# Transposing attention weights with 128 instead of 120 weight columns, in a kernel whose work order is planned

## The chip, the core and the metric

The kernel runs on one core of a Trainium2 chip. A core has five engines with queues of their own: TensorE (PE in the profile, its weight loads are PEld), VectorE (DVE), ScalarE (ACT), GpSimd (POOL) and SyncE (SP, which here only issues transfers). The metric is the device time of one execution, in microseconds; lower is better.

## The reference

Two layers of each kind are interleaved on a sequence of 2048 tokens of width 512. The B layers are gated feed-forward layers of width 1792. The A layers are attention over segments of 32 tokens with 32 heads of 128, in which 8 memory tokens are carried from segment to segment:

```python
for s in range(n_seg):                                 # 64 segments, one after another
    xs = x[:, s * seg_len:(s + 1) * seg_len, :].copy()
    h = jnp.concatenate([mem, xs], axis=1)             # 8 + 32 = 40 tokens
    q, k, v = (einsum('btd,dhe->bhte', h, W) for W in (Wq, Wk, Wv))
    scores = jnp.einsum('bhqe,bhke->bhqk', q, k) * scale
    scores = jnp.where(mask[None, None], scores, -1000000000.0)
    p = _softmax(scores, axis=-1)
    o = jnp.einsum('bhqk,bhke->bhqe', p, v)
    o = jnp.einsum('bhte,hed->btd', o, Wo)
    mem = o[:, :M, :].copy()                           # memory for the next segment
    outs.append(o[:, M:, :])

x = x + A(layernorm(x));  x = x + B(layernorm(x))      # twice, with the same weights
```

(The lines are cut and joined; B is `(sigmoid(x w_gate) * (x w_up)) w_down`.) All data is bf16. The memory makes the segments of one A layer a sequence: segment s + 1 can't start before the output of segment s is there.

## The kernel before

**Steps.** The two A layers run interleaved. Step t treats segment t of the first A layer (job 0) and segment t - 6 of the second (job 1), so that there are 70 steps; steps 6 to 63 hold both jobs, the first six and the last six one alone. With both, 2 x 40 = 80 token columns are moved at once. After every fourth segment of a job, `ffn` treats the block of 128 tokens.

**Inside a step** (`emit_step`) the 32 heads come in six groups: four groups of six heads, one of six and one of two. A group of six of the first kind is two units of three heads; the fifth group is three units of two, the last one unit of two. For a group:

- Q and K are projected (L988), copied by ACT (L999, recorded at L1354) into `qku`, and multiplied to scores (L1023), keys of both jobs on 80 partitions.
- DVE adds the mask (L1037), takes the maximum (L1042), subtracts it (L1044); ACT takes the exponential (L1047); DVE sums (L1049), inverts (L1051) and multiplies (L1054) into `pb`, which is P: 80 rows, 40 columns a head.
- PE transposes P, one transpose a unit (`ptr`, L1067). The part of `pb` that is transposed is the stationary operand, so it is a weight load of 120 columns (three heads) or 80 (two heads); an identity of 80 columns is streamed past it.
- ACT or DVE spread the transposed rows into the block diagonal of `ptsb` (`spread`; L1346, L1348, L1354, L1356), the second and third head of a unit scaled by a column of `third`.
- PE multiplies `ptsb` by V (L1096) and the result by Wo into the bank WB (L1114), which all groups share.

**V.** The rows of V that don't depend on the memory are computed in blocks ahead of time (`v_pass` L778, `v_half` L815), copied into a staging tile and stored to DRAM (`scr`); each step loads the rows that it needs (L956, on SP) into `vsb`. The rest comes from `strips` (L902) by way of the staging tile `sst` (L968). At the start ("boot") the nine buffers of the feed-forward weights (`bootp`: wd, wg, wu) serve as staging tiles of 1024 columns, so that two pieces of 512 columns go into one tile (`k % 2`), with one store on SP or POOL (L793, recorded at L1350) behind the second.

**Order.** Everything is first recorded as a task: `pl.add(engine, cost, function, r=reads, w=writes, lat=...)`. `plan` runs a list scheduler over the 13,975 tasks: each has a cost in ns on its engine, `lat` is the time from its end (for a transfer, to its landing) until a user may go on, and at each moment an engine takes the ready task with the highest priority. The priorities are a list, `SEQUENCE`, packed in a string. The order that comes out is the order in which instructions are issued to each engine's queue; costs, latencies and planned times only shape that order. The waits in the program follow from which data the instructions touch. `warm` adds dummy matmuls where the plan has PE idle (L1340).

**Tiles.** `small` (61 fp32 columns) holds the layernorm sums, the softmax maxima and sums, `third` and other columns; `pb` (three buffers of 80 x 240) and `ptsb` (three of 128 x 680) are tiles of their own. `clear` sets `pb` and `ptsb` to zero once, on POOL.

Of the kernel before, what the change touches and what calls it, by code (L numbers as in the profile page):

```python
# [13 lines left out]
BF16 = mybir.dt.bfloat16  # L14
# [22 lines left out]
def mm_ns(n):  # L37
    return max(n / 2.4 + 2.5, 25.0)
# [23 lines left out]
;B75Pja>jU4U0pOM;*^MkbpH|%}4?Fg>}|j_Fe7An;0dBeihs~taRn~*1imyzs@MXBB0R9K{Dc(essuqm5vjVegY*#r;3xolo=*#1-?ZH8=!ZCdaFMf*a0}ivGjrbTwV#|upXo{Y+?axDr**4ycd`tV!a~o(^lb%  # L62
-d|rO0+fqgdAdzr&+KSQpq8AAQ0*bllqpd%tvRevJpxStQ^W4S_){6dW#yJY_W`r1E@FT2Uxe=|!7W;bJ)tl3672YV;FGR|DVkd^Z9mDZBU)|qz2vb)qec+qgR*uDfG(ABjQYg#!?>2ziThP3XJZ<7By}~T(MF*<
qmF#e8nAJ}ma5RRDM7n7!Nb*c#+B$l%NH_ohW(|Y6t=QIcKkF^gv<Ke0ElUlBE9Awhgg*r9z=q;UHs@XrLpn@^8STeZZpm4rYySV*A{`qe~i<=3=~}!a;!pmPIV4X0*myhJ8NM#8ZFT@lN3|sSL2RXU<MCM+=h3F
cUZtl1!cT4repZ2<a?7UOm;}eEcf1!9rU_qV9&joq!S>>G3~FaMh<O(&UUfQVJI;f>^4JS;D@BZ=ob$IV_U%(f}kMh?;ZR}K^`wxqux*PG;*O^h1ePrUE@nQ1@pKNjOnb@T<n5=h5Q7U)>ARO%)8N?R-z43f`hxu
+4<KMxhgcXLZh50zaR+``nWDvV-O3WIZ4Vj<BEn77tAgGG=~sz#LUy<|B#Lon1R^o_rI!MsvGkS_dZ78f4T}8IN#F-9wHSF%PIz7icWaJ4b@_n?S_W=>Fyp*`-u0QTY~^QPL=2~HW%F9o7rnLuhw{BDtJ}0wAvp*
>XmY-_MUDI?z*N!+72rFAXZww1+mn*!%y}5WMpwR?x4bSBcQK&1}P$VCH1FD^z*R7N_)S*T8UL7(59LW(nrkm+c3)tBWq(KN+pyFi}^NKK{Oc(695<~=YS=47k-}m!dOmUoc-~*P+Z(Y>tmXpp4aDvJ7r7p{1lSM
u9X|gIzGqGsuc|58KKIQH%j@r5l~dgqOrl|jnti3iaN8`w+vOj=t|+GmVm!O!ZRS?Gu%}Q*?|KbSryjiPzgVcoND-b??<=*mO{%qQ07lLnP}xvOB3Y{!~g4cdPK%7>L4i$Y9rV?tH%~;<YQ{`d#MMNH%)gPR&B$J
$Kx3;1Kalf&T2<)yrx~RW5hY=okh1t`vlxrVvm7*(t)*f-$TAkhr`S#w32=A#mr7Ibv|5zLDxLLRDU5561vE^wFhS`SYRnL#0jewffrZ2DBE1j^-aJG*6?H2hN_!{(Ya(cN+pX(4lOtXWOZ<KU%w4T+vAk+Q|CQr
+JBLZ@Wm?nY{e&+)JZS%pSix!b%<MckD^^LWV+rrcVgJ8Q-sqhLUDP)SDG&xeCUe%Ek_nkn$qR4%KI?Mhv9s2OAEmvMj$^-C`#gPbQCB7aZ%8(pvfa$lIZTnhji>N=Ve~^E}+mf#@;`5pK_R_ssCXTb72k6s!Qy2  # L70
Nl-HISA;yjHF-m>59MpPS`ebyqBOEi!Ep!qj@F3W5oWp5(6ZX2W73)u=ETUw$#LTVlLf<6eq2+Qy_sx*@txAt*NG(WJwNxh5P!7QZ6bNCaxLh@x&L6|Ad)L*Hh1yspW5K}ADaAn-2kQip}V9z1$;|e^_f_;d!7TQ
1%k?83~9`7E6Cm-Xr-(^DPf-`NN~2QW$OA%7a6z@+LtI)lwMqAl!t{ADJbWWFU<iWwp~cF`u)edOR%fWX_H>{O;(l`eGH3oa;~f(1nf0%0nu8BFCIdoIJ08c`}5%)^uV^DuFI(8$RYGbh0;Oo^394tSke1#G?bmu
kGfsucMtzFMi|ZuLu#Il4#rb*|J^r2YXt!mtOQW{MqE6cu1<LI;mw6g?O}g{lDqwgT+aa<GEfdx@xWPXYOIaMuK)I5oS4*~)XnW^Ke$*ys?)g;f8OyF{#6HCWyN)YduxAno>0aMm)lb7uZz#GEC+&lIY?76n#|L<
OA^MwN5<fyEuD4J3mv$dgbPa*N?*UwbVf_iq{zrI+&2J=GEIlma^Yfkb%cGcPCf<^(`85Iq=?w`??NAz#_l{>5xBr>!OVc)YBH`8>4Yd0d;{<pqm&=9DLbe0mz1Jyr^g)?_)s7j#W>-M9b?W60n-6cfWdAvGq*9Q
&Byd+WNK?rw+k@X#6qd?h{M;_aWm$*XQKfrX*eg?@~kI2&n3sYewY?T{J7(sA0E)TL?7wm);~OlR4ru7bF5g@1*yHpKKG_yB^}Z*ZH`*|0%H=2G)$Je6P8=zj}K$cDjNrBtIyjk=<&Z+b%M8M5H_@3mv`Y{gP4OR
4cgk}x2MybXqXI8T;wOVv1Hs>2dcRFe7<YS6H1^sMTYLrAL1|T&{PQ2u#T%->p&RQVaqpzMY{W3M7TZ0F<d0*d-rJTGYpAV9dKK!06|9hVvk_>Cz+%Or`;H6%?&+vXT36+a@PX0et1<EdwDr>Q|<OGRUZ-%hjEO}
k348PGh4Bv;N|)M=&8xnDp0=&@1#tSX_sF%ftuu^{mSsvt8dHG`nH2n90W>>+yHheyYv>3HONuWoPw8kQ@(vVmM+O#3#0#92G8s^>}(H$=f^uhUk^~=)zqJTmHw<|d<nld=($9vP~<$zkIr;(-dSI)isKvBw+ljE
?a*kR%(2jkH>AS4h}-*Sg_gCbZSof3D|Z696L#Q>Imqwe&G9_COS+DNZB0l%<@JyDGO(2n9@0W+;$8KNW{y{-r2k_|z4-^+HKJ8zo&3rHM<lJk;o@IvDp)ImjKu$izeCO$yW5DeRTvxU_jC5%%7R@}$+1*wMppQJ
U=;|4m@-@NYK=xqeE{58QTiDD%%W~wx1(RwuV5m&5|WeT5RCH<n*b#}!7e53%Lu{;VY}4e*(j{~dol)%DmpJZ8N6q2c*-j5v$smiOfbhQwxRG%D-CG5dlogMAoXm8$foMd`vL%<YafLq+;nd)l_y_qQwT#f<be}2
zh9_t_+Dc9wGv5|k>U+)*T%+zk`>YP!d(TBz7FV0e3earS;o28kDhG3luC&;i!cQ^*04vOS;kLcq?9a}rumn_uI6bWY}=MkLapbcf-z0_y0f40I>Kn0HH*aR{Fl~AVR3OO+ThgRV3L+3$4tPr)95L7TY7hAt0ebS  # L80
KGmY(!Jcq;A~dE+wRm1lKTqn2jb<&n-dV}dZ+`_;Jc}CQ<gn{cCW`Gq*E6UH$mFnRqt*7T#NbqTL3e}QD6-Oa0X%qw(_Y%aV$Lb<QRM__(w*3fPI&SO00BEv(c59EMNt+gaK4Zuf@ymO<-+##br*f+fH6-{dRBGY
9vKZ1&sa++b*<(=HJD9w<1lWjc2q>u{EI-k@WML0SbO2!;=TYsw`3+8xC~hG$WU`P&;*QSya^m&Ca|BQEmIYU++Crhl#+{j9q}$}i{WH0AGW=Fo2i%Y6Ew*4fPq4d%7i%tW6{H{Y3Wnq9Ol;IbUoUbwX4R4%bSsJ
&&gCiA()`I_M|Wx*}t|^Y<?)GV{M!j%#*{L5=~}SBA*^ge^h8DuP&c(ZR0ToFYP5;heN23-<56(4+|x{i($r&VIos5<JN5LmmET`ji0Z7PYNhY)My$?V@J15i%@eW<pJ+>qM_=T1h-w~&Q%HbC<F6{Tl^8Anp84u
7s;^7jAHamv&>I>*k<`gPKW+5+i1EMEl+pt6i*0`JM~fu8$oIaruqa9^Rg4a!O$*v{HIB;Bkyq79qz)^c+n8CvXEns6VE7EGf0{7%g;crn*d~S{n|0E3342om1T=7rFWc5Uawo7MwRZPy&i$hv|3dfH@w0;=f#F^
Z1tM;Uq$v9F|g08fm^yF6A}M`KL?YzqZ&N7D@Lc&_0A?v*S;?rj);Hp4yaArh8W4<I2oB#c~QkraeRi#I=ATf8~-U5lVKVo{3P_`H#xp=>;KbB>y)GV@A;%p_W!RMU+1Zp3R_e^eB<i1)x{D|hs}cw>E^%PtS^+3
2=+g+sowjML0P${9xg|CNN?kZVblt>M0(jn)$rYg<|YBK=o7Mz92~J`x`XV11L3FWsFL3Nu)k)vI_}N;szu!KN;CQ!i{D4!G2ZNL(>j-7nMG85h?l!bW2%D5l0?4GMBekT&_p9mG7n^iQbML~b7Daz?>CaVwURe*
l!B~;_{SE&z7shn<(Uz7F$fU0R@`bVqGQ&b+QU}70qYin9#f&?+PbR%&k&<{y&}~jdAGiee~dRVbYIY#n}Q&lX=m$05ah!)a(X*{EVR`&XJ>|Vz9ZoVcu-lZ1!l^nYh5OE^`X^L6`~jwZcTUCuM>&FaDr5(G)|%a
{pfOKR6Vhm!u>r6;^ZEB9)Ggz9-ku2u`j^IR#!>K3I9`*Ilz?+3NmSJ8C5zIxqRF*mvPTsU+wL2AGZxOKyw(}zx!Jjr}#D-l)gxA`wt2)tJv>RV}^X%7%zvCZSDiq?|0<2YSgL1z$Uu;M9@I`2$sxtO(aEW6IgOe
FUBMieS(?pPa!g`TN#==1r&TT>-fx&gCl?Xj8){T`x&yu`5us4XH3dY6%KIJK5$vS(rO~L<G?-ew|Vt?YB`3xZaz*RUONm$8&m`{Ks8;CfLbboJtYMr4rn}{I^stUcXyX~^e~z9l4SR%g&;>e>F(w~SeDg(aaQ2Z
&tD-Czi`2w<PI9*lEE!XVyv`;j#*(W<0(qftXYTpcLK46suXruoUI@$#{Qp9?omqCgCBjoFA#t+Lq&#8wXOtvDWJ38)|&~<Th_R}rn>h(({G<2uH|mHhP+QZ?@bG12C-;+29WEP)dCr<!jmF*d@ihJD>l3M%DD(Z  # L90
j+pZplYMEQK85F=Qd7Kx?EW?k62)~0L6MpRg>H2<@&rUT{%JBPfQ<g7;uul`l}X`MVkxeYN7McMYKD$0+2E8IqK5s6pCc7+CuOxpf|tkXtf)df6n!<^-G1Od%!hCaF#5H%p(6avkc|G~Bwf}arSSB7(hKsc<pulp
%_ZMqlc+l?ZNysSW-XO5a+HTDAaOuo$MOb1tc-^ky!_+NFn|VWwr;a{$e}9Pj(`_lhXUfW6P=zLtQWUX+zLOvaT88KEfQaY?Y|CFwL#3cunkY-Vteop$weuTdr01l8Q}IF^$9tZ-c?nmU#YM2g+3MXgwW#ynOAL0
m-9(pu0LF36=4$V)Xvxm4E48<Z7%+y8s~Oy7+BlYneIGy9l_Cj3|WF})i5qAtQ}@;(-aJ=O!%bQdu}w89-@6W9wG?GgtfO<2iLLV927-iSza1{BJwWok|+V%j8LfPAU-ci@6+G5W##{ds)Mmsa;p;5vRm!{c(kt_
!LEBmGgy#<uvgvRu$v1egBOO`lhZh)`Y^y=8?Z($VdV0U9)YMIz|66Q=$!SU+D+z}*EwH9lSAKT;w+(WyMWlV>I1MFFD-Z96gG$Lf1L*4pt-`XZcEo1e2;Mt(c$<I(6WD5ED}L5au!kM#21yBFU29PU-fU4@ey3G
&Lmeqv#lb^@Zo-VqurwOCu`(3q@G8Cu9=iO(fVRh-(+t&InT3Iowlxh+qF<5TR@yDyQ2eeC2JzC7DnCA@yG<uwXobge2yPgkoQYkx&V7CNd{#Txw)2kwM8`_81VG(2szd2gT#Vwub7-dD<%M2IAN5-QqpedJ>Mjy
a!x}}c)Nm|54q#BARV%X2a*L%0m*Fd(EPUXf91b-zLyOTp5-vth^6M2Et_{A*V|pEvJfx7R1X&M3mL0na&PF>BkUI}Mj)3#&I+$9H-D<S;XNnDx$$p%YGKHY9<ZkTF%1gt{c9`~jQ553WwJUP0ca}X8gg!Sc&<tc
TlD;(wxlQhW)>_8xJr=imo$q`Oxyg%oUKpATw79S`b&c*s9Q`8@pT%$EMtZbY|&B}COebJljqF&uUVW5jqZKZ3?#<iFF9L2oZKKDp_U96!4+NfOHe08^3LB`si{czzQU*IRCH8bAG`Bq0rT+=vbO!O|F>Q_euU>*
j%a|?kO7^s0~NOv+#S27_`A-+{Q6w#0Z=<B%Q@CdU<k`p`#*9!PY2p5kkO|l%x`SKXI~N~(Na)q_T0F23t+FTThf+4(n91#{AR`61#hDo<h0=aN}Ji_{yKb%fwrn49M@1{mV{n;t2O^q@CeS>Uwzr7)P9rMi&H;o
s~bdolUo?=aUpX?^S87FOj68T@c}Ru?HMraHa?+eR@WS&3)bOT|LNzR&u`wD!TCFYULJhzTP~RP|HQYEvt+t1;KP?eIuahlHr?xPf>#@B?*yj8NdX65F=#m^m@Z(I!unr;YwWP`rqpUlui`A37Bs#tE&%+Fp|>s|
D8XcEf|Hwg^(U7`-Z(KSsjXPX%A6hpZ+2>-htRfPzB&6+U3mrRBom^NBm;+6>zhA_2~71qP(LmnlXNW~t71T@MOyG)$4TViO~fxg4q)Nt9;E9JPMokhdzH|Y1Cp;FGCTc#%4?S~j%?lKP{@%Ky`7Ynd>cki!P%OO  # L100
2FF{spr}K29{qIn^~Ac*Y3pbraUP}zu)I<9)o1rl!~ncy(B}L7XCrv_84{n}SKBooG4s3d#gqIpGjb0?5xNBNI%XyZ#M_EvF}inxv*W?NSG66s-VWn0P0X<|Mp62mLFoN~Gr%IOiSNC>tJZ_)3Ku~$>mObw0MUnv
S;-B9Zrh7q#jzB~iVjW0ejWH_v7I{)?w+*3Rqg#+5y6HLS4t!_vDWUea^>lmqvLTgMAW)c@1)+x7#h%`?BbwiJ_N^DAWC4R-`411?e<0~9;)^?6hOsx5$+PRVm)&NYtnO<GR?z@g~s7h4p1R#f?at|6p%I{*+W{_
URx{&6s#4_h@RIy@2fU)rl3C5Ts~?LpQ~^&C7*h!Y(y~}$sSxQ;}HkK+VopD#EKUz)VM=r*n8ELu)DO*#yR>B(>K$LJlz6NLUY<R)TWCXK7xt?ymkH5G-*1(5%_(K$oL{4ZrDG918Eh?wS%_D@oR_C$p1M%@gnEZ
N~=6=Pim;h9#A)@I~r2*N1c*9q$0}1x<hL$F2-L-CAtVP$WMG0W}NBCAyhg0V6}1kJM1c8WPM~SOHorktqsd$Y*!oYOlux5Jpr?%`sP+>Ii@?a04RZ9u{237Gx@89qZ_1Iq66QjJU%GM{5~7#vK#wHB*9MkFx3HC
# [1315 lines left out]
```

## Time and profile before

| | |
|---|---|
| time, median of 3 runs | 1793.92 us (1793.05 to 1796.88) |
| the profiled execution | 1789.87 us, with a span of 1788.0 us from first to last instruction |
| PE, PEld busy | 1752.0 us, 1512.2 us |
| DVE, ACT, POOL busy | 1182.3 us, 1179.3 us, 578.6 us |
| granted TensorE clock, mean | 0.999 |
| transposes of P (L1067) | 840, of which 560 with 120 weight columns and 280 with 80 |

"Busy" is the time in which an engine had an instruction in work. Matmuls are pipelined, so that each one's duration (about 200 ns) is much longer than the distance to the next one's start; a matmul's cost in a dense stretch is that distance. A line of a group reads: line of the kernel, engine, operation, what it writes and reads, shape, count, then busy time in us and mean duration in ns, then the idle time of the engine ahead of it and what ended it.

### The profile page before, as it was taken

How to read it: one execution, taken by the hardware profiler on the slowest of the kernel's cores; microseconds unless marked ns; L12 is line 12 of the kernel's file. 1: busy time of each engine (PE TensorE's matmuls, PEld its weight loads, DVE VectorE, ACT ScalarE, POOL GpSimd, SP SyncE). 2: the span in 40 equal slices, each digit the busy share in tenths (PEclk: the TensorE clock that was granted, in tenths of full speed). 3: DMA queues.
4: the chain of work that ended last, by engine and by line, in shares of the span. 5: the costliest groups of instructions: out<-in, count | busy, mean ns of one | idle time of the engine just before them, and what ended most of it. 6: DMA issues, size and time to landing. Idle time of an engine off the chain costs nothing.

```text
span 1788.0 us, 91153 instructions
## 1 busy us (share of the span) xinstructions
PE 1752.0 (98%) x39103; PEld 1512.2 (85%) x39311; DVE 1182.3 (66%) x4076; ACT 1179.3 (66%) x3243; POOL 578.6 (32%) x837
## 2 busy tenths in 40 slices
PE   9999999999999999999999999999999999999998
PEld 4588788888888898989888898889888888889886
DVE  3367676776677667766776677667766765667675
ACT  4667777766666666666666666666666766666564
POOL 5412132422333242323324231333325231333432
PEclk9999999999999999999999999999999999999999
DMA  9735354634555463545546454556546454554543
GB/s 340 255 98 141 106 162 131 188 106 141 156 165 159 132 191 109 159 127 166 158 133 194 137 154 111 148 161 167 157 128 197 116 149 120 161 155 135 165 137 100
DMA packets 144752, 273.39 MB, mean 153 GB/s; under 512 B 34306, under 2 KB 82314, under 8 KB 144346
## 3 DMA queue, kind: packets, MB, share of 16 engines
q0 software_dynamic: 56720, 183.22, 35.1%
q1 hardware_dynamic: 87626, 84.31, 16.7%
q8 instruction: 308, 5.05, 1.2%
q14 instruction: 98, 0.80, 0.1%
HBM read 221.78 MB, written 27.07 MB: 139 GB/s over the span
## 4 chain that ended last, share of the span: by engine, by line
PE 89%; ACT 3%; DVE 2%; issue 1%; SPq 1%; DMA 1%; POOL 0%; DVEq 0%; ACTq 0%; POOLq 0%
PE bank L988 32%; PE bank L1114 17%; PE bank L1216 10%; PE bank L902 7%; PE bank L778 6%; PE bank L1023 4%; PE bank L1096 4%; PE bank L1239 4%; PE bank L1067 2%; PE bank L738 1%; DVE st L1037 1%; PE bank L1340 1%; SPq L968 1%; ACT ptsb L1346 1%; PE bank L1184 1%
## 5 line engine op out<-in xcount | busy, mean ns | idle before, releaser
L988 PE MATMUL bank<-hT,wq_sb 128*128 128x80 bf16 (+3 forms) x8960 | 615.5, 198 | 1.2
L988 PE MATMUL bank<-hT,wk_sb 128*128 128x80 bf16 (+3 forms) x8960 | 615.2, 198 | 0.8 <-issue 0.8
L1354 ACT CAST qku<-bank 128x480 bf16<-128x480 f32 (+3 forms) x770 | 380.7, 507 | 215.5 <-PE bank L988 185.1
L988 PEld LDWEIGHTS <-wq_sb 128*128 128x128 bf16 x8960 | 453.4, 99 | 23.3 <-issue 11.7
L988 PEld LDWEIGHTS <-wk_sb 128*128 128x128 bf16 x8960 | 447.0, 99 | 1.0 <-issue 1.0
L1037 DVE TENSOR_TENSOR st<-bank,cst 40x240 f32<-40x240 f32 (+3 forms) x768 | 278.9, 368 | 163.3 <-PE bank L1023 152.6
L1114 PE MATMUL bank<-otsb,wo_sb 128*128 128x80 bf16 (+1 forms) x8960 | 358.6, 198 | 1.6 <-ACT otsb L1354 0.2
L1114 PEld LDWEIGHTS <-wo_sb 128*128 128x128 bf16 x8960 | 336.5, 99 | 13.5 <-issue 0.9
L1209 POOL DMA_DIRECT2D wu<-in_B_w_up_dram x217 | 164.0, 756 | 273.6 <-PE bank L1216 126.5
L1208 POOL DMA_DIRECT2D wg<-in_B_w_gate_dram x217 | 163.9, 756 | 256.4 <-PE bank L1216 181.9
L1354 ACT CAST otsb<-bank 128x480 bf16<-128x480 f32 (+3 forms) x420 | 198.3, 483 | 52.3 <-PE bank L1096 35.4
L1233 POOL DMA_DIRECT2D wd<-in_B_w_down_dram x217 | 153.7, 709 | 207.4 <-PE bank L1023 71.8
L1346 ACT ACTIVATE ptsb<-bank,small 80x160 bf16<-80x160 bf16 (+5 forms) x477 | 169.5, 379 | 27.7 <-PE bank L1067 23.9
L1047 ACT ACTIVATE st<-st 80x240 f32<-80x240 f32 (+3 forms) x420 | 159.7, 383 | 29.0 <-DVE st L1044 25.6
L728 POOL TENSOR_TENSOR small<-small 128x1 f32<-128x1 f32 (+1 forms) x80 | 44.8, 563 | 402.1 <-DVE small L727 400.0
L1216 PE MATMUL bank<-xnT,wg 128*128 128x128 bf16 (+2 forms) x1784 | 172.0, 219 | 0.6
L1216 PE MATMUL bank<-xnT,wu 128*128 128x128 bf16 (+2 forms) x1784 | 171.0, 218 | 0.0
L1049 DVE TENSOR_REDUCE small<-st 80x6 f32<-80x240 f32 (+3 forms) x420 | 151.2, 362 | 24.5 <-ACT st L1047 22.8
L1023 PE MATMUL bank<-qku 128*128 128x80 bf16 (+1 forms) x2240 | 165.4, 198 | 0.7
L1044 DVE TENSOR_TENSOR st<-st,small 80x240 f32<-80x240 f32 (+3 forms) x420 | 154.4, 369 | 3.4
L1054 DVE TENSOR_TENSOR pb<-st,small 80x240 bf16<-80x240 f32 (+3 forms) x420 | 153.8, 369 | 4.2
L1042 DVE TENSOR_REDUCE small<-st 80x6 f32<-80x240 f32 (+3 forms) x420 | 151.8, 363 | 4.3
(104 smaller groups left out, 2405.3 us busy)
## 6 DMA issues: line engine op xcount, KB each, us to landing
wg<-in_B_w_gate_dram POOLq DMA_DIRECT2D x220, 256.0 KB, 4.4
wu<-in_B_w_up_dram POOLq DMA_DIRECT2D x220, 256.0 KB, 4.4
wd<-in_B_w_down_dram POOLq DMA_DIRECT2D x220, 256.0 KB, 4.3
vsb<-scr SPq DMA_DIRECT2D x345, 48.0 KB
vsb<-sst SPq DMA_DIRECT2D x372, 32.0 KB
scr<-vst SPq DMA_DIRECT2D x112, 96.0 KB
vsb<-scr SPq DMA_DIRECT2D x230, 24.0 KB
wv_sb<-in_A_Wv_dram SPq DMA_DIRECT2D x8, 512.0 KB
```

The costliest lines, as they stand in the source:

```text
L988: nc.tensor.matmul(o_ap, lhsT=W[:, c, h * P:(h + 1) * P], rhs=mv(c), start=(c == 0), stop=(c == DC - 1))
L1023: nc.tensor.matmul(s_all(SB)[:, w0 + i, :], lhsT=fview(qku[:, i, 0, 0:1], [(1, P)]), rhs=qku[:, i, 1, 0:ncol], start=True, stop=True)
L1037: pl.add("DVE", dve_ns(n, True), lambda gsz=gsz, hs=hs, st=st, SB=SB, pj_=pj_, npj_=npj_, mk=mk, idx=idx: nc.vector.tensor_tensor(out=st[p ...
L1044: pl.add("DVE", dve_ns(n), lambda gsz=gsz, hs=hs, st=st, mx=mx: nc.vector.tensor_tensor(out=st[pr, hs], in0=st[pr, hs], in1=mx[pr, hs].uns ...
L1047: pl.add("ACT", act_ns(n), lambda hs=hs, st=st: nc.scalar.activation(out=st[pr, hs], in_=st[pr, hs], func=ACTF.Exp, scale=self.scale), r=s ...
L1054: nc.vector.tensor_tensor(out=pb[pr, hs, 0:L], in0=st[pr, hs], in1=rs[pr, 0:gsz].unsqueeze(2).to_broadcast([npart, gsz, L]), op=ALU.mult)
L1114: nc.tensor.matmul(WB[:, c * ncol:(c + 1) * ncol], lhsT=self.wo[:, h, c * P:(c + 1) * P], rhs=otsb[:, hl, 0:ncol], start=(h == 0 and c == ...
L1208: pl.add("POOL", 760, lambda wg=wg, fs=fs: nc.gpsimd.dma_start(out=wg[:], in_=self.wgv[:, :, fs]), r=[("wo", self.H - 1)], w=[gk] + bt, la ...
L1209: pl.add("POOL", 760, lambda wu=wu, fs=fs: nc.gpsimd.dma_start(out=wu[:], in_=self.wuv[:, :, fs]), r=[("wo", self.H - 1)], w=[uk] + bt, la ...
L1216: nc.tensor.matmul(gu[:, 2 * i + k, 0:n], lhsT=W[:, c, i * P:(i + 1) * P], rhs=xnT[:, c, rw], start=(c == 0), stop=(c == DC - 1))
L1346: nc.scalar.activation(out=dst, in_=src, func=ACTF.Copy, scale=by)
L1354: nc.scalar.copy(out=dst, in_=src)
```

## The change

The tiles `small`, `pb` and `ptsb` become parts of one tile, `pbt`, of which each `pb` has 248 columns instead of 240. A transpose of three heads takes 128 columns of `pb` as its weights instead of 120: the eight further columns are the first of the next unit, or for the second unit the eight added ones, and the eight rows that come out more are not read. Transposes of two heads keep their 80 columns. In `v_pass` the first piece of a staging tile writes a key, and the second reads it, which puts the two in sequence in the plan. The stores of the boot are planned to land 6.0 us after their end instead of 5.0 us. The string `SEQUENCE` is replaced by another list of the same 13,975 tasks.

```diff
 SEQUENCE = r"""
-...
+...
 """
@@ setup_tiles
-        small = c.tile([P, 61], F32, name="small")
...
-        self.pb = [c.tile([LW, HG, L], BF16, name=f"pb{i}") for i in range(3)]
-        self.ptsb = [c.tile([P, 17 * L], BF16, name=f"ptsb{i}") for i in range(3)]
+        np_, nt_ = HG * L + P - 3 * L, 17 * L
+        pbt = c.tile([P, 3 * (np_ + nt_) + 2 * 61], BF16, name="pbt")
+        self.ptsb = [pbt[:, nt_ * i:nt_ * (i + 1)] for i in range(3)]
+        self.pb = [pbt[0:LW, 3 * nt_ + np_ * i:3 * nt_ + np_ * (i + 1)] for i in range(3)]
+        small = pbt[:, 3 * (np_ + nt_):3 * (np_ + nt_) + 2 * 61].bitcast(F32)
@@ v_pass
-            pl.add("PE", DC * mm_ns(512), vmm, r=keys + [("wv", h) for h in range(4 * k, 4 * k + 4)], w=[B], use=[vs])
+            own = ("own", len(pl.bufs)) if k % w == 0 else own
+            pl.add("PE", DC * mm_ns(512), vmm, r=keys + [("wv", h) for h in range(4 * k, 4 * k + 4)] + [own] * (k % w), w=[B] + [own] * (k % w == 0), use=[vs])
@@ v_pass and v_half, the stores
-                       ..., lat=3000.0 + 2000.0 * boot,
+                       ..., lat=3000.0 + 3000.0 * boot,
@@ emit_step, pmul
-                nc.vector.tensor_tensor(out=pb[pr, hs, 0:L], in0=st[pr, hs],
+                nc.vector.tensor_tensor(out=pb[pr, 0:gsz * L].rearrange("p (h k) -> p h k", k=L), in0=st[pr, hs],
@@ emit_step, ptr
-                pt = PB[0:w * L, 0:nu * LW // 2].bitcast(BF16)
+                m = P if w == 3 else w * L
+                pt = PB[0:m, 0:nu * LW // 2].bitcast(BF16)
                 for ul in range(nu):
-                    nc.tensor.transpose(out=pt[:, ul * LW:(ul + 1) * LW], in_=pb[full, w * ul:w * ul + w, :].rearrange("p i k -> p (i k)"),
+                    nc.tensor.transpose(out=pt[:, ul * LW:(ul + 1) * LW], in_=pb[full, w * L * ul:w * L * ul + m],
                                         identity=self.ident[full, full])
```

## The prediction

> **What bounds the kernel now.** I read the page first, then the stages, the groups by form, the timeline of one stretch, and the waits of the start. Page: span, busy time, and the shares of the chain that ended last.
>
> ```profile
> span 1788.0 us, 91153 instructions
> PE 1752.0 (98%) x39103; PEld 1512.2 (85%) x39311; DVE 1182.3 (66%) x4076; ACT 1179.3 (66%) x3243; POOL 578.6 (32%) x837
> ...
> PE 89%; ACT 3%; DVE 2%; issue 1%; SPq 1%; DMA 1%; POOL 0%; DVEq 0%; ACTq 0%; POOLq 0%
> ```
>
> PE is busy 98% and carries 89% of the chain. That alone doesn't say that a faster PE ends sooner, so I look at the stages (PE, PEld, DVE, ACT and POOL busy, granted clock, DMA share, GB/s):
>
> ```profile
> 0.00:100.00 100.00, 92.26 (x1082) 50.96 (x1094) 40.61 (x140) 54.87 (x138) 45.67 (x100) 0.98 0.85 283
> ...
> 300.00:1600.00 1300.00, 1284.88 (x28467) 1141.45 (x28631) 880.52 (x3010) 867.19 (x2260) 431.49 (x597) 1.00 0.53 151
> ```
>
> From 300 to 1600 us PE is busy 1284.9 of 1300 us at a clock of 1.00. As matmul durations overlap, I checked it by the distances from one matmul's start to the next's, over all records (distances that are a missing record of 216 ns left out). A 128x80 matmul with 128 columns of weights follows the last one after 35.8 ns, one of 128 columns after 56, one of 512 after 216. What exceeds these by over 40 ns is 16.8 us between 300 and 1600, 7.8 us in the first 100 us, 9.5 us from 100 to 300, and 8.0 us after 1600: 42 us in all. The long middle is a bare sum of PE's start distances; the two ends hold its waits.
>
> Next, weight loads by form (mean ns is the number ahead of the last bar):
>
> ```profile
> L1067 PEld LDWEIGHTS <-pb 80*120 80x120 bf16 x560 | 55.7, 134 | 9.6 <-DVE pb L1054 1.9 <-DVE st L1044 0.4
> L902 PEld LDWEIGHTS <-hT 128*32 128x32 bf16 x2272 | 54.1, 96 | 53.0 <-issue 1.7 <-DVE hT L1127 0.6 <-ACT oxT L1354 0.4
> L1096 PEld LDWEIGHTS <-vsb 80*128 80x128 bf16 x512 | 28.9, 98 | 5.5 <-issue 1.0 <-DMA vsb<-scr 0.2
> L1067 PEld LDWEIGHTS <-pb 80*80 80x80 bf16 x280 | 22.2, 118 | 4.2 <-DVE pb L1054 0.9
> L1239 PEld LDWEIGHTS <-hff 128*96 128x96 bf16 x14 | 1.4, 122 | 1.7 <-DVE hff L1222 1.1
> ```
>
> 32, 80, 96 and 120 columns take 96, 118, 122 and 134 ns: (134 - 96) / 88 = 0.43 ns a column. 128 columns lie off that line, at 98 ns on the same 80 rows. The reader is to see that the 560 loads of P (four groups of heads, two transposes each, 70 steps) are the slowest form of the table, by 36 ns. Whether that reaches the end shows in the timeline of PE (start, duration):
>
> ```profile
> 804.84 0.27 PE L1023 MATMUL bank<-qku 128*128 128x80 bf16 x3
> 804.94 0.28 PE L1067 MATMUL bank<-cst,pb 80*120 80x80 bf16 x2
> 805.05 0.32 PE L988 MATMUL bank<-hT,wq_sb 128*128 128x80 bf16 x4
> 805.20 0.31 PE L988 MATMUL bank<-hT,wk_sb 128*128 128x80 bf16 x4
> ```
>
> Three score matmuls take 0.10 us to the next start, the two transposes 0.11 us, although all stream 80 columns.
>
> Last, the waits between 36 and 58 us (us in total, times, longest), and the landing of the start's V stores:
>
> ```profile
> ACT wg L1354 <- DMA scr<-wg: 5.5, 1, 5.5
> ACT wd L1354 <- DMA scr<-wd: 4.7, 1, 4.7
> PE bank L778 <- ACT xvf L1354: 3.5, 1, 3.5
> PE bank L778 <- ACT wg L1354: 1.0, 1, 1.0
> ```
>
> ```profile
> DMA to landing us min/median/max: 2.0/5.3/7.2
> ```
>
> Twice ACT stands before a copy into a staging tile whose old store hasn't landed. V banks then stay full, and PE stops: start distances exceed theirs by 1.19 us at 40.7 and 3.62 us at 53.7, half of what the first 100 us lose. The plan reckons with 5.0 us to landing; half of the stores need more than 5.3.
>
> **The change, part by part.** The sum is made on the profiled execution (1789.87 us for a span of 1788.0). The median of the runs shown is 1793.92, 4.05 us above; I carry the difference to the median.
>
> **Transposes of threes.** Nothing is added: 560 loads of 120 columns become loads of 128, the matmul still streams 80 columns. Bound above by the slope of the slow rows: 8 x 0.43 = 3.4 ns, x 560 = 1.9 us slower if 128 columns stay slow. Below, by the row of 80 rows x 128 columns (L1096): its 80-column matmuls follow each other after 36.2 ns in mean. The 548 transposes that have a next record within 60 ns of theirs lose 7.55 us against 35.8 ns, 13.8 ns each: the second of a pair starts 50 ns after the first (median), the next instruction 55 ns after the second. Against 36.2 ns it is 7.3 us, for 560 some 7.5 us. Here two sections of "TensorE: Matmul & The Clock Gate" in the Trainium skill differ. "LDWEIGHTS" gives a time in proportion to the columns alone, P / 1.2 ns, which speaks against the change: an estimate of 6.7 ns for 8 columns, 3.7 us over 560, slower. "Weight-path perf modes" says that a fast load is taken when there are exactly 128 weights and the type isn't FP32, which gives the 7.5 us faster. The rows decide for the second (98 ns on the same 80 rows against 134). What no row shows is a 128-column load from an odd place: the new pb buffers begin every 496 bytes, the second transpose 240 bytes on; the 128-column loads shown start at multiples of 64 bytes in their tiles. [...]I keep the near row.
>
> How much reaches the end: 5.1 us of it lies between 300 and 1600, where PE waits 16.8 us in 1300; I count 0.9, as a step's hand-over (the transposes of L1184 wait on ACT for the last oxT) doesn't shorten with PE. The other 2.4 us lie where a step alone waits for its own chain: three quarters. 4.7 + 1.8 = **6.5 us**.
>
> The eight new output rows are read by nobody (L1346 to L1356 still take 120). POOL clears 248 columns a buffer instead of 240, beside the first weight loads: nothing.
>
> **One tile for pb, ptsb and small.** Same instructions and bytes. The risk is a wait between parts that don't overlap. The nearest case is small itself: POOL writes one part of it (L728), DVE others 420 times each (L1042, L1049, L1051), and line 1042 shows no idle time ahead of it at all. cst is shared likewise. So nothing; if regions were not told apart, DVE's P would wait for the transposes of another group, 420 times at a fraction of a us, over 100 us. I leave that out of the range.
>
> **Pieces in sequence, stores later.** The "own" key adds no instruction and no wait, only an order in the plan: nothing by itself. The longer landing (6.0 us, above the median of 5.3, below the longest of 7.2) makes the plan pick another staging tile or do other PE work first. At best both stops go, 4.8 us. But the DMA engines are busy 0.85 in that stretch, and a tile used later pushes a V piece, its ACT copy and its SP or POOL store back. If no PE work is ready in its place, nothing is won, and one more wait like that of 1.19 us, or two, may come: +2. Between -4.8 and +2 I take **-3 us**, near the end that the trace names. Next late after this would be V rows from DRAM (297.5 us: 1.7 us of PE).
>
> **Another order.** Every priority is rewritten. Decoded and set against the order that the plan of before gives, PE's tasks between 200 and 1600 us move by one place in the median (nine of ten by up to 6), those of the first 100 us by 26, of the second by 9, after 1700 by 5. ACT and POOL look alike, DVE moves by 5 to 10 places throughout; SP's loads and stores move by 1 to 3 places in the median, nine of ten by under 20. So the middle stays, and start and end are laid anew. It can win a part of the 9.5 + 8.0 us that PE waits there, and lose as much; nothing in the trace of before shows which: **0**, +-4.
>
> Sum: 6.5 + 3 = 9.5 us; 1793.92 - 9.5 = 1784.4, told as **1784**.
>
> **The rivals.** Where PE waits anyway, a faster PE only waits more. *Hidden:* if the steps of the middle were bound by the chain through DVE and ACT, the transposes would give a third, 2.5 us, and the start 3: 1788.4. For it: L1184 waits of 0.5 us at block ends. Against: 98.8% busy there, DVE and ACT 68 and 67%. *Slow load:* odd addresses or 80 rows deny the fast load: 1.9 us lost, 3 won, 1792.8. For it: no such address in the trace. Against: 98 ns on 80 rows. *Order wins:* a laid-anew start and end give back 8 of their 17.5 us beyond the stop at 53.7: 1776.
>
> *Slower:* SP's queue is in order, and carries V's stores (L1350) as well as the loads of V rows that the P times V matmuls (L1096) await (L956, L968). If the new order puts loads behind stores that wait for their copy, these rows come late. The chain shows what one costs: "DMA vsb<-sst" at 295.85 us, of which PE lost 1.71. Such stops must use up the 6.5 us first (the start then wins nothing), and 3.6 more; from six new ones on it is slower by over 0.2%, at seven 1793.9 - 6.5 + 12 = 1799.4. Against it: SP's order moves by 1 to 3 places in the median, and only three such waits stand among the longest pieces of the chain.
>
> **How the numbers follow.** 0.2%, 3.6 us, is about what a measurement of this kernel can tell from no change. The forecast 0.62 (0.02 of it within 0.2%), order wins 0.12, hidden 0.12 (0.02 within), slow load 0.06 (all within), slower 0.08. Faster 0.60 + 0.12 + 0.10 = 0.82, same 0.10, slower 0.08. The range takes full gain and order (7.5 + 4.8 + 4 = 16.3, a little more for order wins: 1775) and the slow load's 1792.8, so 1775 to 1793; outside lie the slower case and the tail of order wins.
>
> **What would show it.** Right: P's loads of threes at 98 ns instead of 134, the transposes' distances near 36 ns, PE busy between 300 and 1600 as high as now with that stretch's work done some 5 us sooner; ACT's waits on scr<-wd and scr<-wg gone before 60 us. Wrong: loads at 137 ns; the same 98 ns but PE's waits grown by 5 us; new waits on vsb<-scr or vsb<-sst; waits between DVE pb and ACT ptsb that share no data.

## The result, and the profile after

| | before | after |
|---|---|---|
| time, median | 1793.07 us (1784.54 to 1797.11, 20 runs) | 1788.57 us (1786.39 to 1793.41, 20 runs) |
| the profiled execution | 1789.87 us | 1789.13 us |
| PE's weight loads of three heads, mean of one | 134 ns | 99 ns |
| ACT busy | 1179.3 us | 1201.9 us |

The ratio is 0.998, interval 0.9971 to 0.999: the changed kernel is faster by 0.2%, some 3.6 us of 1793 (the medians lie 4.5 apart). The forecast was 9.5 us. The time lies in the range, the direction is right, and more than half of the gain is missing. The two profiled executions differ by 0.7 us only, because the one of before was 3 us quicker than its median; they serve to see where time goes, the ratio to say how much.

The page of the changed kernel, its span, busy times and the shares of the chain that ended last:

```profile
span 1787.1 us, 91201 instructions
...
PE 1765.1 (99%) x39305; PEld 1505.1 (84%) x39305; DVE 1184.6 (66%) x4075; ACT 1201.9 (67%) x3244; POOL 579.0 (32%) x837
...
PE 90%; ACT 4%; DVE 3%; DMA 1%; issue 1%; SPq 1%; DVEq 0%; POOL 0%; ACTq 0%; POOLq 0%
```

PE still sets the time. (That it is busier by 13 us says little: the trace of before holds 39,311 weight loads but 39,103 matmuls, so some 200 matmul records are missing there; here both are 39,305.) The number to stop at is ACT's. Its work is nearly the same copies and spreads (3244 instructions against 3243), and it is busy 23 us longer.

The stages (PE, PEld, DVE, ACT and POOL busy, granted clock, DMA share, GB/s):

```profile
0.00:100.00 100.00, 96.90 (x1266) 55.49 (x1267) 47.39 (x165) 63.15 (x169) 46.54 (x101) 1.00 0.87 289
...
300.00:1600.00 1300.00, 1291.98 (x28499) 1131.30 (x28495) 880.56 (x2994) 879.47 (x2242) 426.82 (x591) 1.00 0.53 150
```

In the first 100 us PE is busy 96.9 us instead of 92.3 and passes 1267 weight loads instead of 1094: the start is denser. The granted clock of these 100 us is 1.00, where before had 0.98; the experiments come back to that. In the middle there is 12 us more of ACT, and 136 weight loads *fewer* in the same 1300 us. So the start gains, and the middle gives back.

The weight loads of P by form, and the start's waits of ACT for staging tiles (us in total, times, longest):

```profile
L1033 PEld LDWEIGHTS <-pbt 80*128 80x128 bf16 x560 | 40.8, 99 | 12.8 <-DVE pbt L1019 4.0 <-DVE st L1009 0.4
L1033 PEld LDWEIGHTS <-pbt 80*80 80x80 bf16 x280 | 22.0, 118 | 4.9 <-DVE pbt L1019 2.2
```

```profile
ACT wg L1320 <- PE bank L742: 2.0, 6, 0.4
ACT wd L1320 <- PE bank L742: 1.8, 5, 0.5
ACT wu L1320 <- PE bank L742: 0.9, 3, 0.5
ACT wg L1320 <- PE bank L780: 0.7, 1, 0.7
ACT wu L1320 <- DMA scr<-wg: 0.3, 1, 0.3
```

The loads of 128 columns take 99 ns instead of 134, although they begin at odd places. The two waits of 5.5 and 4.7 us for V's stores are down to one of 0.3 us. Both things that the prediction reckoned on have happened. Something else costs time, and it shows in ACT's timeline. Two spreads of three heads, one right behind the other, are one entry "x2"; start and length of the pair stand in front. First a pair of before on ACT and one on DVE, then after:

```profile
703.18 0.67 ACT L1346 ACTIVATE ptsb<-bank,small 120x160 bf16<-120x160 bf16 x2
...
747.43 0.50 DVE L1348 TENSOR_SCALAR ptsb<-bank,small 120x160 bf16<-120x160 bf16 x2
```

```profile
699.82 0.81 ACT L1312 ACTIVATE pbt<-bank,pbt 120x160 bf16<-120x160 bf16 x2
...
744.15 0.63 DVE L1314 TENSOR_SCALAR pbt<-bank,pbt 120x160 bf16<-120x160 bf16 x2
```

A pair takes 0.14 us longer on ACT and 0.13 us on DVE. The groups hide it, because an instruction's own duration has not changed (line, engine, operation, shape, count | busy, mean ns | idle before, releaser), before and after:

```profile
L1346 ACT ACTIVATE ptsb<-bank,small 120x160 bf16<-120x160 bf16 x172 | 66.8, 392 | 7.5 <-PE bank L1067 6.1 <-DVE ptsb L1356 0.5
```

```profile
L1312 ACT ACTIVATE pbt<-bank,pbt 120x160 bf16<-120x160 bf16 x176 | 68.9, 395 | 7.6 <-PE bank L1033 3.8 <-DVE pbt L1016 0.3 <-DVE pbt L1322 0.2
```

392 and 395 ns. In before, two durations of 392 fit in 0.67 us, so they overlap by some 0.11; in after two of 395 take 0.81, with no overlap left. I therefore measured, over all spreads that directly follow a spread on their engine, the distance from the end of the one to the end of the next (medians in ns; 160 columns are a spread for both jobs):

| | before | after | e3_pack_only | e5_ptsb_apart |
|---|---|---|---|---|
| ACT, 120x160 | 290 | 426 | 427 | 291 |
| ACT, 80x160 | 280 | 422 | 423 | 290 |
| ACT, 40x160 | 172 | 317 | 318 | 173 |
| DVE, 120x160 | 208 | 337 | 336 | 208 |
| DVE, 40x160 | 143 | 267 | 267 | 142 |

(The last two columns belong to the experiments.) The cause stands in the program. Among the instructions that spread, ACT has 325 of 752 that wait for an earlier instruction of *ACT itself*, where before had 26 of 737; on DVE it is 96, where before had none. In before two spreads write two tiles, or parts of one tile that the program tells apart. In after all three `ptsb`, all three `pb` and `small` are parts of one tile, and the spreads get waits on each other.

The trace of after separates the two kinds within this one tile, when an engine's instructions are set beside the program's in order. Of the 98 spreads of 120x160 on ACT that follow a spread, the 89 with a wait on ACT end 426 ns after it (median), the 9 without such a wait 284 ns. On DVE all 59 of 160 columns have the wait; the spreads of 40x80, of which none has it, stay at 102 ns as in before.

### The profile page after: what moved, and what is told of

Read it like the earlier page. It is cut to its first block, busy times and chain, and to the rows that moved or that the text cites. A ratio compares the mean times of both kernels' runs of the same rounds, so it can differ in the third digit from the quotient of the medians.

```text
span 1787.1 us, 91201 instructions
## 1 busy us (share of the span) xinstructions
PE 1765.1 (99%) x39305; PEld 1505.1 (84%) x39305; DVE 1184.6 (66%) x4075; ACT 1201.9 (67%) x3244; POOL 579.0 (32%) x837
## 3 DMA queue, kind: packets, MB, share of 16 engines
q1 hardware_dynamic: 87658, 84.38, 16.8%
## 4 chain that ended last, share of the span: by engine, by line
PE 90%; ACT 4%; DVE 3%; DMA 1%; issue 1%; SPq 1%; DVEq 0%; POOL 0%; ACTq 0%; POOLq 0%
PE bank L953 31%; PE bank L1080 16%; PE bank L1182 10%; PE bank L742 7%; PE bank L867 7%; PE bank L1205 5%; PE bank L988 4%; PE bank L1062 4%; PE bank L1033 2%; ACT pbt L1312 1%; PE bank L1306 1%; DVE st L1002 1%; PE bank L702 1%; ACT qku L1320 1%; PE bank L1150 1%
## 5 line engine op out<-in xcount | busy, mean ns | idle before, releaser
L1320 ACT CAST qku<-bank 128x480 bf16<-128x480 f32 (+4 forms) x770 | 379.7, 507 | 211.4 <-PE bank L953 173.4
L1312 ACT ACTIVATE pbt<-bank,pbt 80x160 bf16<-80x160 bf16 (+4 forms) x488 | 181.6, 381 | 27.5 <-PE bank L1033 18.0
L692 POOL TENSOR_TENSOR pbt<-pbt 128x1 f32<-128x1 f32 (+1 forms) x80 | 45.3, 568 | 391.3 <-DVE pbt L691 390.7
L1014 DVE TENSOR_REDUCE pbt<-st 80x6 f32<-80x240 f32 (+3 forms) x420 | 151.4, 363 | 29.9 <-ACT st L1012 27.3
L1009 DVE TENSOR_TENSOR st<-st,pbt 80x240 f32<-80x240 f32 (+3 forms) x420 | 154.5, 369 | 3.3
L1019 DVE TENSOR_TENSOR pbt<-st,pbt 80x240 bf16<-80x240 f32 (+3 forms) x420 | 153.8, 369 | 4.3
L1007 DVE TENSOR_REDUCE pbt<-st 80x6 f32<-80x240 f32 (+3 forms) x420 | 151.9, 363 | 4.2
```

What stands on the lines that cost most here:

```text
L1009: pl.add("DVE", dve_ns(n), lambda gsz=gsz, hs=hs, st=st, mx=mx: nc.vector.tensor_tensor(out=st[pr, hs], in0=st[pr, hs], in1=mx[pr, hs].uns ...
L1019: nc.vector.tensor_tensor(out=pb[pr, 0:gsz * L].rearrange("p (h k) -> p h k", k=L), in0=st[pr, hs], in1=rs[pr, 0:gsz].unsqueeze(2).to_broa ...
L1312: nc.scalar.activation(out=dst, in_=src, func=ACTF.Copy, scale=by)
L1320: nc.scalar.copy(out=dst, in_=src)
```

## The experiments

Theory W: the one tile adds waits of ACT and DVE on their own earlier work, and these eat the gain. Rivals: O, the other order loses in the middle what it wins at the start; H, a transpose that is done sooner shortens nothing there. The four kernels ran on one chip beside before, whose median on it was 1797.0 us (1791.53 to 1803.86, 17 runs). Percentages are ratios to before, and us are per cents of 1797.

### e3_pack_only: before, with the one tile and nothing else

The order, the landing time and the transposes are those of before; `pb` has its 248 columns, of which a transpose takes 120. As an edit of the changed kernel (cut):

```diff
-                m = P if w == 3 else w * L
+                m = w * L
 SEQUENCE, lat and keys: as before
```

> The kernel before with pb, ptsb and small as parts of one tile, and nothing else: 120 weight columns, old order, old landing. In the program 302 spreads on ACT and 100 on DVE then wait for an earlier instruction of their own engine. Theory W (these waits eat the gain; after, one ACT spread ends 420 ns behind another in place of 285): slower than before by 3 to 7 us, 1796 to 1800. Theory O (the new order in the middle eats it) and theory H (the middle is bound by the softmax chain anyway, so a faster PE only waits more): no change, 1793 +-1.5.

Measured: 1809.87 us (1805.23 to 1814.17, 6 runs), ratio 1.0063 (1.0038 to 1.0088): **slower by 0.6%, some 11 us**. PE, SP and POOL get the same instructions in the same order with the same waits as in before; only the waits of ACT on ACT and of DVE on DVE differ. O and H have nothing to say to such a loss. W has the right sign and too small a size. The pair of spreads, and then the stage of the middle:

```profile
710.79 0.81 ACT L1349 ACTIVATE pbt<-bank,pbt 120x160 bf16<-120x160 bf16 x2
...
757.02 0.63 DVE L1351 TENSOR_SCALAR pbt<-bank,pbt 120x160 bf16<-120x160 bf16 x2
```

```profile
300.00:1600.00 1300.00, 1275.45 (x28056) 1128.04 (x28218) 877.73 (x2982) 874.65 (x2229) 424.34 (x588) 1.00 0.53 149
```

The same 0.81 and 0.63 us, and PE gets through 28,218 weight loads in the 1300 us instead of 28,631. What PE waits for fits spreads that end later. First before, then e3_pack_only (us in total, times, longest):

```profile
PEld L1096 <- issue: 5.6, 10, 1.7
...
PEld L1067 <- DVE pb L1054: 2.8, 9, 0.5
...
PE bank L1096 <- DMA vsb<-sst: 1.8, 2, 1.5
```

```profile
PEld L1099 <- issue: 11.3, 32, 1.7
...
PE bank L1099 <- DMA vsb<-sst: 7.4, 5, 2.6
...
PEld L1070 <- DVE pbt L1056: 4.7, 17, 0.5
```

Transposes wait more often for DVE's P, and P times V (L1099), the user of the spread rows, twice as long. ("issue" names no releaser, so that it is the spread which holds P times V is argued, not shown.) The rows of V by way of `sst` come late too; I take it that the step's timing has shifted against its loads.

### e1_t128_old_order: the one tile and the wide transposes, in the old order

As an edit of the changed kernel (cut):

```diff
 SEQUENCE: as before
-                       ..., lat=3000.0 + 3000.0 * boot,
+                       ..., lat=3000.0 + 2000.0 * boot,
-            own = ...; r=... + [own] * (k % w), w=[B] + [own] * (k % w == 0)
+            r=..., w=[B]
```

> The change without its plan: 128 weight columns and the one tile, with the old order, no sequence key and the old landing. W: the transposes' 6.8 us less what the one tile costs, 1790 to 1794. O: 1786.5, the full gain of the transposes, as the old order fits. H: 1790 to 1792, a third of it.

Measured: 1801.82 us (1797.83 to 1808.47, 12 runs), ratio 1.003 (1.0014 to 1.0045): slower than before by 0.3%, with the fast weight loads in it. Against e3_pack_only it is 0.33% faster, 6 us by the ratios and 8 by the medians: the wider transposes pay even here, which speaks against H, and less than the tile costs.

### e5_ptsb_apart: the changed kernel, with the spreads' targets as tiles of their own

Everything of the change stays, the order too; only the three `ptsb` leave the shared tile. (To make room, `small` is cut to 54 columns: the layernorm's reciprocal is written over sums that are no longer needed, and three constants lie in spare columns of the third `pb`. So `pb` and `small` still share a tile.)

```diff
-        pbt = c.tile([P, 3 * (np_ + nt_) + 2 * 61], BF16, name="pbt")
-        self.ptsb = [pbt[:, nt_ * i:nt_ * (i + 1)] for i in range(3)]
+        self.ptsb = [c.tile([P, 17 * L], BF16, name=f"ptsb{i}") for i in range(3)]
+        pbt = c.tile([P, 3 * np_ - 8 + 2 * 54], BF16, name="pbt")
```

> The changed kernel with ptsb as three tiles of its own (pb and small share one, two columns of the layernorm sums are reused in place): no spread waits for its own engine, PE's and SP's programs are the same as after's. W: faster than after by 3 to 7 us, 1782 to 1785.5. O and H: like after, 1788.5 +-1.5.

Measured: 1780.98 us (1778.67 to 1783.44, 6 runs), ratio 0.9906 (0.9886 to 0.9926): **0.9% faster than before**, and the fastest kernel here. PE, SP and POOL have the programs of the changed kernel down to the waits, and the spreads' waits on their own engine are back at before's 26 on ACT and none on DVE. So O falls: the same order that had won 0.2% wins 0.9%. The pairs are short again:

```profile
702.40 0.67 ACT L1313 ACTIVATE ptsb<-bank,pbt 120x160 bf16<-120x160 bf16 x2
...
739.03 0.49 DVE L1315 TENSOR_SCALAR ptsb<-bank,pbt 120x160 bf16<-120x160 bf16 x2
```

and in the middle ACT's busy time falls back to that of before (867.2), with 28,672 weight loads against 28,495 in after:

```profile
300.00:1600.00 1300.00, 1282.36 (x28506) 1135.83 (x28672) 878.03 (x3010) 867.69 (x2255) 426.50 (x590) 1.00 0.54 150
```

The same waits of PE, in after and then here:

```profile
PEld L1062 <- issue: 9.1, 32, 0.9
...
PEld L1033 <- DVE pbt L1019: 6.2, 25, 0.4
```

```profile
PEld L1063 <- issue: 7.5, 17, 1.0
...
PEld L1034 <- DVE pbt L1020: 3.1, 11, 0.4
```

The transposes' waits for P halve. DVE writes P into the shared tile in both kernels, so that this half has nothing to do with the tile P lies in; it fits that what runs ahead of P on DVE and ACT is done sooner.

### e6_apart_old_order: separate targets and wide transposes, in the old order

The tiles of e5_ptsb_apart, the order, landing time and keys of e1_t128_old_order: what the wide transposes bring by themselves. (`pb` and `small` share a tile here too; PE, SP, POOL and ACT have before's waits, DVE 13 more.)

> 128 weight columns with ptsb apart, in the old order and with the old landing: the transposes alone, without the waits. W and O: 1786 to 1787, the 6.8 us that the start distances of the transposes lost in the trace after. H: 1790 to 1792.

Measured: 1787.97 us (1785.73 to 1791.26, 6 runs), ratio 0.9946 (0.9926 to 0.9967), 9.7 us faster (6 to 13). ACT's waits of the start stand here as in before,

```profile
ACT wg L1358 <- DMA scr<-wg: 5.4, 1, 5.4
ACT wd L1358 <- DMA scr<-wd: 3.8, 1, 3.8
```

so they belong to the old plan, and their end in after belongs to the new one.

### What the four say together

Each part is measured more than once, in us by the ratios (to 1797). The last column takes only executions with a mean granted clock of 0.999 (medians of 2 to 6):

| part | from | us | at clock 0.999 |
|---|---|---|---|
| wide transposes | e6 against before; e1 against e3 | -9.7; -6 | -8; -10 |
| new plan (order, landing, pieces in sequence) | e5 against e6; after against e1 | -7; -9 | -6; none |
| one tile | e3 against before; e1 against e6; after against e5 | +11; +15; +13 | +15; +13; none |

The sum -9.7 - 7 + 13 = -3.7 has to close, as each step starts where the last one ended; what the table shows is that a part comes out alike from different pairs. (After was not measured beside e5 and e1: before's median was 1793.07 us beside the one and 1797.0 beside the others. By the medians after - e5 is 7.6 us, by the profiled executions 8.5, so that its +13 could be 8.)

Why the clock: before's 17 executions here have a mean clock between 0.995 and 1.000, and take 1803.86 us at the one end and 1791.53 at the other. The trace of before shows where a part of it goes. PE stands from 53.7 to 57.5 us at the V matmuls (the second of the two stops), and in the 3.4 us after 57.0 (busy times, clock, DMA share and GB/s as in the stages above) the clock is 0.50:

```profile
57.00:60.40 3.40, 2.89 (x7) 1.04 (x8) 0.41 (x1) 1.46 (x4) 2.65 (x5) 0.50 1.04 364
```

Seven V matmuls follow each other there after 393 to 427 ns instead of 216, which is 1.4 us. The clock of the first 100 us is 0.98 in all four kernels with the old plan and 1.00 in after and e5. So a part of what the new plan wins is the clock that it keeps.

The milestones show when. Each time is that of the k-th copy of the memory tokens, with which a step lets the next one start (us, one profiled execution each, so that 2 or 3 us mean little):

| | before | after | e3 | e1 | e5 | e6 |
|---|---|---|---|---|---|---|
| 1st | 93.1 | 85.3 | 93.6 | 92.9 | 84.8 | 92.8 |
| 13th | 358.9 | 353.1 | 363.1 | 359.7 | 351.0 | 358.0 |
| 61st | 1583.0 | 1581.4 | 1603.2 | 1592.4 | 1572.5 | 1580.3 |
| last | 1752.2 | 1750.2 | 1773.9 | 1761.6 | 1742.0 | 1748.2 |
| 13th to 61st | 1224.1 | 1228.3 | 1240.1 | 1232.7 | 1221.5 | 1222.3 |

The new plan leads by 8 us at the first copy. With the one tile it loses the lead on the way (1228.3 for 48 steps); with `ptsb` apart it keeps it (1221.5). The kernels with one tile need 1228 to 1240 us for the same steps, the others 1221 to 1224.

How do 13 us come out of 0.14 us? Of the spreads of 160 columns in after that directly follow another, 255 on ACT and 59 on DVE have the wait: 255 x 0.14 + 59 x 0.125 is some 43 us of the two engines, of which less than a third reaches the end. What of it is PE standing can be counted: stops of over 40 ns between 300 and 1600 us are 24.1 us in before and 42.3 in e3, 37.2 in e1 and 25.8 in e6, 28.8 in after and 25.2 in e5. (They are counted a little more finely than in the prediction, by streamed columns, so that before stands at 24.1 instead of 16.8.) Of these, stops that a step of the softmax or a spread ended are 2.0 and 8.1 us, 9.6 and 2.8, 8.6 and 2.8: +6 us each time. Late V rows add 8.6 us in e3 and little in after. The rest I have not assigned.

Not tried, and open: the new order with 120 columns, and the new order with the old landing, so how the plan's -7 us divides is not known. Nor were the waits put by hand on separate tiles. That the waits, and not the buffers' new addresses, lengthen a pair is shown by the spreads within the one tile (426 ns with the wait, 284 without). That this is what costs the 11 to 15 us follows from the programs, which differ in nothing but own-engine waits and addresses.

## Why the prediction was right and wrong

**Transposes of threes: right, and sized too low if anything.** 99 ns where it expected 98. The second of a pair starts 40 ns after the first in the median (before 50), the next instruction 35 ns after that (before 55); small losses of PE over the span fall from 15.95 to 9.15 us, 6.8 less, 4.6 of it in the middle. Counted were 6.5 us; e6_apart_old_order has 9.7 (6 to 13), which holds 6.5 at its edge, and 8 at equal clock. (A slip in the working, 5.1 at 0.9 being 4.6 and not 4.7, changes nothing.) The rule that speaks against the change (the Trainium skill, "TensorE: Matmul & The Clock Gate", "LDWEIGHTS": a time in proportion to the columns, by the estimate 3.7 us slower) has lost against the row, and the odd offsets did not matter.

**Pieces in sequence and stores later, -3, and another order, 0: right in sign, too small.** Together -7 (e5 against e6; -9 in the packed pair). The two long waits on `scr` before 60 us went, and no new stop of that size took their place. The term counted the stops alone, 4.8 us at best. The half clock behind the second one, 1.4 us, was not in it, though the 0.98 of the first 100 us stood in the stages; the two together are 6.2. The rival of V rows that come late by SP's order did not happen: between 300 and 1600 us, 1.6 us of PE's stops are ended by DMA in after, 1.2 in before.

**One tile: the step that failed.** "The nearest case is small itself: POOL writes one part of it (L728), DVE others 420 times each (L1042, L1049, L1051), and line 1042 shows no idle time ahead of it at all. [...] So nothing." It is +11 to +15 us in the old order, and 8 to 13 in the new one. Three things are wrong in it. The row is not near: the parts of `small` are plain runs of columns, while a spread writes every third block of 40 columns of a `ptsb`, between the blocks of the two other spreads. (Which writes are told apart in the shared tile was not found out. On ACT 296 of the 508 spreads with four such blocks have a wait on ACT, and 7 of the 163 with two; into a `ptsb` of its own the same four blocks get such a wait 12 times of 507.) It looks at idle time ahead of the line, and a wait for the engine's own last instruction leaves hardly any: it only takes away an overlap. In before's program 407 of the 420 instructions of that very line 1042 wait for DVE itself, and no idle time shows. And the bounds were nothing, or "over 100 us" if regions were not told apart at all, which was then left out; between the two lies a tile whose parts are told apart nearly everywhere, and the case that decided. The last sentence of the prediction had named a sign of the right family, waits "between DVE pb and ACT ptsb that share no data", but on the wrong pair: they were between one spread and the next. Its sign before that came as it was written, the fast loads "but PE's waits grown by 5 us": in the middle they are 28.8 us instead of 24.1.

**The sum.** With the tile's 13 us beside its own other terms, -6.5 - 3 + 13 would have given +3.5, slower; with 8 us, -1.5. That the kernel came out faster by 3.6 is due to these two terms, each too small by some 2 to 4 us. The direction was right partly by luck, by errors that cancel.

**What would have priced it.** A page of the Trainium skill bears on the DVE half, "VectorE: DVE Perf Modes", and it points both ways. Its section "The DRAIN you can't avoid" reports eight copies that took as long with a semaphore after each as with one at the end: by that the waits cost nothing. The same section says that a next instruction which is not held starts earlier. The trace decides for the second statement: one DVE spread ends 208 ns after another without the wait, 337 with it.

## What to carry to other kernels

Putting buffers into one tile is an edit of the program's waits, not only of its memory: before it is costed at nothing, list the waits of both programs engine by engine, own-engine waits too. Such a wait does not show as idle time or as a longer instruction; look at the distance from one end to the next, or at a run of instructions in the timeline (x2 in 0.67 or in 0.81 us). And where a change has several parts, a small net result can be two gains and a loss: here keeping all of it but the packing of `ptsb` took 0.9% instead of 0.2%.

## What was new about the hardware

- A spread that waits for the spread before it on the same engine ends 426 ns after it instead of 290 on ACT, and 337 instead of 208 on DVE. The added 0.12 to 0.145 us is nearly the same for 40, 80 and 120 partitions: it is an overlap of start and end that is lost, not work (one of 120x160 on ACT takes 392 ns in before and 395 in after).
- A weight load of 128 columns takes 99 ns on 80 rows, also when it begins 240 bytes into a buffer whose pitch is 496 bytes.
- The trace can lack some 200 matmul records in one kernel and none in the other, which moves PE's busy time by more than the effect looked for; weight loads in a window (28,495 and 28,672) were the better measure of progress.
- A stop of PE of 3.6 us in the old plan is followed by 3.4 us at a granted clock of 0.50, with matmuls of 512 columns 427 ns apart instead of 216. The traces of the new plan, without the stop, show 1.00 there.
